# Reordering the first batch's loads and norms in a cross-covariance attention kernel with a folded feed-forward part

## The chip, the cores and the metric

The kernel runs on one core of a Trainium2 chip. The time is the device time of one execution in microseconds (us). Six runs of the kernel before have a median of 585.03 us (584.68 to 585.35). The profile was taken of one execution of 584.84 us, in which the core's span is 583.0 us; the rest, 1.84 us, lies around the span.

Names: PE is TensorE (matmul), PEld its weight load, ACT is ScalarE, DVE is VectorE, POOL is GpSimd, SP is SyncE. L207 is line 207 of the kernel before.

## The reference

Attention runs over channels, not tokens, for each of 4 batches of 5824 tokens and 256 channels; the feed-forward part has no nonlinearity beyond a product.

```python
qn = q / (np.linalg.norm(q, axis=1, keepdims=True) + 1e-06)   # norms over the tokens, one per channel
kn = k / (np.linalg.norm(k, axis=1, keepdims=True) + 1e-06)
s = kn.transpose(0, 2, 1) @ qn / tau                          # 256 x 256 per batch, tau = 1
a = softmax(s)                                                # over the last axis, 1e-9 added to the sum
x = (v @ a).reshape(B * S, D)
out = (((x @ w1) * (x @ w2)) @ w3) @ w_out
```

## The kernel before, in words

**Folding.** v @ a @ w1 is computed as v @ (a @ w1): for each batch the 256 x 256 softmax is multiplied into w1 and w2 (`fold`, L291, eight units of two matmuls, each evicted with the softmax's row factor by ACT, L302, or DVE, L304). Likewise w3 @ w_out is made once (`w_unit`). So the main loop over a batch's tokens has three matmul steps: a and b (`emit_ab`, L348), their product (ACT copies a, L360; DVE multiplies, L362), and the output (`emit_out`, L367). A batch has 12 chunks of 512 tokens (the last of 192), and eight feature blocks j per chunk. v must be transposed first: by DMA from SP, or, for the first two pieces of batch 0, on PE (L121), with a copy by ACT (L123) or DVE (L125).

**Scores.** q and k come in six pieces a batch: pieces of 8 slots of 128 tokens, the last of 5 slots and a remainder of 64 tokens. `load_piece` (L95) issues them on POOL's queue, which converts f32 to bf16. Four buffers each hold q and k (L63), so the fifth piece waits until PE is done with the first. For batch 0 nothing else can run yet: `first_scores` (L194) takes each slot with six matmuls, two for the scores G (L207, 256 columns), two for q^T q (L211) and two for k^T k (L215, 128 columns each); the last two give the squared norms on their diagonals. For batches 1 to 3 the scores are spread over the batch before by an agenda (`score_units`), with the squares taken by ACT and added up by DVE.

**Softmax units.** `soft_units` (L220) makes the norms, the row of k factors on all partitions, the scaled scores, the exponentials, the sums, and the folds. For batch 0: `norms_first` multiplies the squares by the identity (L225) and sums the rows (L227); `rnorm` takes the square root by Ln and Exp on ACT (L248, L249), adds 1e-6 and inverts on DVE (L250, L251); `row` (L256) spreads the k factors by an f32 matmul (L259) and an ACT copy (L265); `scaled` multiplies G by that row (L271) and ACT takes the exponential with the q factor as its scale (L274). For batches 1 to 3 `norms` adds two accumulators on DVE (L232), and `ss` sums over the partitions by four f32 matmuls of one column (L240).

**Order.** The order on each engine is the order in which the program emits; there is no scheduler. Batch 0 runs straight through (L401 to L436). After that, `make_agenda` (L461) gives each side job a due time on a clock of estimated PE time, and `run_due` emits what is due ahead of each `emit_ab` or `emit_out`. The softmax units of the next batch have their due times in L499. In batch 0 POOL issues q and k of a piece in turn, two pieces ahead of PE (L401, L415), then v, w1, w2, w3 and w_out (L417 to L427). The program lets POOL have eight loads under way: the ninth waits for the first to land, and so on.

Of the kernel before, what the change touches and what calls it, by code (L numbers as in the profile page):

```python
# [10 lines left out]
AF = mybir.ActivationFunctionType  # L11
ALU = mybir.AluOpType
F32 = DT.float32
BF16 = DT.bfloat16

P = 128
PIECE = 8
# [6 lines left out]
def kernel(  # L24
# [12 lines left out]
    nc = tc.nc  # L37

    B, N, C = q.shape
    T, D = out.shape  # L40
    F = moe_w1.shape[1]
# [6 lines left out]
    CT = C // P  # L48
    FT = F // P
# [24 lines left out]
    nc.vector.memset(ones_f, 1.0)  # L74
    ones_b = consts.tile([P, 1], BF16)
    nc.vector.memset(ones_b, 1.0)

    w12 = consts.tile([P, CT, 2, F], BF16)
    W_sb = consts.tile([P, FT, D], BF16)
# [12 lines left out]

    pieces = {}

    def load_piece(nm, n, pi, split=False):  # L95
        pool = v_pool if nm == "v" else qk_pool
        t = pool.tile([P, PIECE, C], BF16, tag=nm, name=f"{nm}_{n}_{pi}")
        main, left = qk_main[nm, n]
        g = LAST if pi == NP_ - 1 else PIECE
        if pi == NP_ - 1:  # L100
            if nm != "v":
                nc.gpsimd.memset(t[LEFT:, g, :], 0.0)
            nc.gpsimd.dma_start(out=t[:LEFT, g, :], in_=left)
        cuts = [0, g] if not split else [0, g // 2, g]
        for lo, hi in zip(cuts, cuts[1:]):
            nc.gpsimd.dma_start(out=t[:, lo:hi, :], in_=main[:, pi * PIECE + lo : pi * PIECE + hi, :])
        pieces[nm, n, pi] = t
# [83 lines left out]
                units.append((0.22 if part < 2 else 0.0, lambda pr=pr, part=part: pair_unit(pr, part)))  # L191
        return units

    def first_scores(pi):  # L194

        if pi == 0:
            G_tiles[0] = psum.tile([P, CT, C], F32, tag="G", name="G_0", bufs=1)
            G_tiles["sq"] = psum.tile([P, 2 * CT, P], F32, tag="out", name="sq_0", bufs=3)
        G, S = G_tiles[0], G_tiles["sq"]
        qt, kt = pieces["q", 0, pi], pieces["k", 0, pi]  # L200
        g = PIECE if pi < NP_ - 1 else LAST + 1
        for i in range(g):
            first = pi == 0 and i == 0
            last = pi == NP_ - 1 and i == g - 1
            for ct in range(CT):
                cs = slice(ct * P, (ct + 1) * P)
                nc.tensor.matmul(  # L207
                    G[:, ct, :], lhsT=qt[:, i, cs], rhs=kt[:, i, :],
                    start=(first and ct == 0), stop=(last and ct == CT - 1), skip_group_check=True,
                )  # L210
                nc.tensor.matmul(  # L211
                    S[:, ct, :], lhsT=qt[:, i, cs], rhs=qt[:, i, cs],
                    start=(first and ct == 0), stop=False, skip_group_check=True,
                )
                nc.tensor.matmul(  # L215
                    S[:, CT + ct, :], lhsT=kt[:, i, cs], rhs=kt[:, i, cs],
                    start=False, stop=(last and ct == CT - 1), skip_group_check=True,
                )

    def soft_units(n):  # L220
        st = {}

        def norms_first():
            d = work.tile([P, 2 * CT, P], F32, tag="sq", name="dg", bufs=2)
            nc.vector.tensor_mul(d, G_tiles["sq"], ident.unsqueeze(1).to_broadcast([P, 2 * CT, P]))  # L225
            ss = work.tile([P, 4], F32, tag="ss0", name="ss0", bufs=1)
            nc.vector.tensor_reduce(out=ss, in_=d, op=ALU.add, axis=mybir.AxisListType.X)  # L227
            rnorm(ss)

        def norms():  # L230
            a1 = work.tile([P, 2, C], F32, tag="acc1", name=f"acc1_{n}", bufs=1)
            nc.vector.tensor_add(a1, accs[n][:, 0], accs[n][:, 1])  # L232
            st["a1"] = a1

        def ss():
            m = psum.tile([P, 512], F32, tag="ab", name=f"ss_{n}", bufs=4)
            for w in range(2):
                for ct in range(CT):
                    i = w * CT + ct
                    nc.tensor.matmul(  # L240
                        m[:, i : i + 1], lhsT=st["a1"][:, w, ct * P : (ct + 1) * P], rhs=ones_f,
                        start=(i == 0), stop=(i == 3), skip_group_check=True,
                    )
            rnorm(m[:, :4])

        def rnorm(src):
            r = work.tile([P, 4], F32, tag="r", name=f"r_{n}", bufs=2)
            nc.scalar.activation(out=r, in_=src, func=AF.Ln)  # L248
            nc.scalar.activation(out=r, in_=r, func=AF.Exp, scale=0.5)  # L249
            nc.vector.tensor_scalar_add(r, r, 1e-6)  # L250
            nc.vector.reciprocal(r, r)  # L251
            if inv_tau != 1.0:
                nc.vector.tensor_scalar_mul(r[:, :CT], r[:, :CT], inv_tau)
            st["r"] = r

        def row():  # L256
            m = psum.tile([P, 512], F32, tag="ab", name=f"row_{n}", bufs=4)
            for ct in range(CT):
                nc.tensor.matmul(  # L259
                    m[:, ct * P : (ct + 1) * P],  # L260
                    lhsT=st["r"][:, CT + ct : CT + ct + 1].to_broadcast([P, P]), rhs=ident,
                    start=(ct == 0), stop=(ct == CT - 1), skip_group_check=True,
                )
            kr = work.tile([P, C], F32, tag="kr", name=f"kr_{n}", bufs=1)
            nc.scalar.copy(kr, m[:, :C])  # L265
            st["kr"] = kr

        def scaled():
            s = work.tile([P, CT, C], F32, tag="s", name=f"s_{n}", bufs=1)
# [21 lines left out]
        def fold(i):  # L291
# [11 lines left out]
            else:  # L303
                nc.vector.tensor_scalar_mul(dst, m, st["rs"][:, c1 : c1 + 1])  # L304

        head = [(0.0, norms_first)] if n == 0 else [(0.0, norms), (1.0, ss)]
        return (
            head + [(0.6, row), (0.0, scaled), (0.2, sums)]
            + [(0.43, lambda i=i: fold(i)) for i in range(8)]
        )  # L310


    clock = [0.0]
# [11 lines left out]
    def at(t, cost, fn):  # L325
        seq[0] += 1
        agenda.append((t, seq[0], cost, fn))
# [68 lines left out]
    def load_qk(n, pi):  # L396
        load_piece("q", n, pi)
        load_piece("k", n, pi)


    load_qk(0, 0)  # L401
    load_qk(0, 1)
    masks.make_identity(nc, ident)
    nc.vector.tensor_copy(ident_b, ident)
    w3T = [
# [4 lines left out]
    w3r = moe_w3.rearrange("(jh jl) l -> jl jh l", jl=P)  # L410
    w1r = moe_w1.rearrange("(ch cl) f -> cl ch f", cl=P)
    w2r = moe_w2.rearrange("(ch cl) f -> cl ch f", cl=P)
    for pi in range(NP_):
        if pi + 2 < NP_:
            load_qk(0, pi + 2)  # L415
        if pi + 2 == NP_:
            load_piece("v", 0, 0, split=True)  # L417
            for h in range(2):
                hs = slice(h * F // 2, (h + 1) * F // 2)
                nc.gpsimd.dma_start(out=w12[:, :, 0, hs], in_=w1r[:, :, hs])  # L420
                nc.gpsimd.dma_start(out=w12[:, :, 1, hs], in_=w2r[:, :, hs])
            load_piece("v", 0, 1)
            for h in range(2):
                js = slice(h * FT // 2, (h + 1) * FT // 2)
                nc.gpsimd.dma_start(out=w3_bf[:, js, :], in_=w3r[:, js, :])
            nc.gpsimd.dma_start(out=wout_sb, in_=moe_w_out.rearrange("(lh ll) c -> ll lh c", ll=P))
            load_piece("v", 0, 2)  # L427
        first_scores(pi)
    soft0 = soft_units(0)
    soft0[0][1]()  # L430
    transpose_half_on_pe(0, 0, 0, True)
    for _, fn in soft0[1:3]:
        fn()
    transpose_half_on_pe(0, 0, 1, False)
    for _, fn in soft0[3:8]:
        fn()  # L436

    def w3_transpose(jt):
        pe_transpose(
# [21 lines left out]
    def make_agenda(b):  # L461
# [2 lines left out]
        n = b + 1  # L464
        if b == 0:
            for i in range(4):
                at(0.3 + 0.6 * i, 0.43, soft0[8 + i][1])
            at(7.0, 0.5, lambda: transpose_half_on_pe(0, 1, 0, True))
            at(8.0, 0.5, lambda: transpose_half_on_pe(0, 1, 1, False))
            for jt in range(FT):  # L470
                at((12.0 if jt < 4 else 15.0) + jt, 0.5, lambda jt=jt: w3_transpose(jt))
                at(24.0 + jt, 0.87, lambda jt=jt: w_unit(jt))
            at(14.0, 0.0, lambda: transpose_piece(0, 2))
            loads = [("v", 0, 3, 14.0), ("v", 0, 4, 34.0), ("v", 0, 5, 54.0)]
            loads += [("qk", 1, pi, t) for pi, t in enumerate([22.0, 30.0, 40.0, 52.0, 66.0, 80.0])]
            loads += [("v", 1, pi, t) for pi, t in enumerate([96.0, 108.0, 122.0])]
            t0, t1 = 52.0, 120.0
        else:
            loads = [("v", b, pi, t) for pi, t in [(3, 1.0), (4, 20.0), (5, 34.0)]]
            t0, t1 = 16.0, 104.0  # L480
            if n < B:
                loads += [("qk", n, pi, t) for pi, t in enumerate([4.0, 12.0, 27.0, 44.0, 58.0, 72.0])]
                loads += [("v", n, pi, t) for pi, t in enumerate([84.0, 96.0, 108.0])]
# [12 lines left out]
        for i, (cst, fn) in enumerate(units):  # L496
            at(t0 + (t1 - t0) * i / len(units), cst, fn)
        soft = soft_units(n)
        ts = [t1 + 1.0, t1 + 4.0, t1 + 6.5, t1 + 8.5, t1 + 12.0] + [t1 + 13.0 + 0.9 * i for i in range(8)]  # L499
        for t, (cst, fn) in zip(ts, soft):  # L500
            at(t, cst, fn)
        agenda.sort()
# [50 lines left out]
```

## Time and profile before

| what | value |
|---|---|
| median of 6 runs | 585.03 us |
| profiled execution | 584.84 us, span 583.0 us |
| PE busy | 562.1 us (96% of the span) |
| DVE, ACT busy | 372.8 us (64%), 339.0 us (58%) |
| POOL's queue | 39.46 MB as written, 39.1% of 16 DMA engines |
| PE idle ahead of L207, waiting for k | 12.4 us in 4 waits |
| first score matmul, last score matmul of batch 0 | 8.80 us, 35.43 us |
| first fold matmul, first a matmul | 40.71 us, 43.99 us |

How to read it: the span is the time from the first instruction to the last. An engine's busy share says little where stages have different limits: here PE is busy nearly all the time from about 41 us on, and waits only in the first 41 us. Loads are shown by the bytes that they write (bf16), half of what they read. Rows of a timeline give the start, the length, the engine, the line, the operation and, in brackets, the idle time before it and what ended it. Rows with "xN" merge N instructions. A matmul's length includes its pipeline; the distance from start to start is what it costs.

### The profile page before, as it was taken

The page shows a single profiled execution, that of the slowest core. Times are in us where ns is not written, and L with a number is a line of the kernel's source. Part 1 is how long each engine was busy: PE and PEld are TensorE (multiplying, and loading weights), DVE is VectorE, ACT ScalarE, POOL GpSimd, SP SyncE. Part 2 cuts the span into 40 slices and gives each one's busy share as a digit, 9 for nine tenths or more (in the row PEclk, how much of TensorE's full clock was granted, in tenths as well). Part 3 has the DMA queues.
Part 4 walks back from the last instruction along what each step waited for, and adds up shares of the span by engine and source line. Part 5 has one row for each costly group of instructions (what it writes and reads, how often), then busy time and mean ns, then how long its engine had stood idle before and what let it go on. Part 6 is the DMA issues. An engine that isn't in the chain of part 4 may idle for free.

```text
span 583.0 us, 10194 instructions
## 1 busy us (share of the span) xinstructions
PE 562.1 (96%) x3836; PEld 363.2 (62%) x3840; DVE 372.8 (64%) x552; ACT 339.0 (58%) x617; POOL 68.5 (12%) x145
## 2 busy tenths in 40 slices
PE   3779999999999999999999999999999999999996
PEld 3654576766666666666665766666665765566555
DVE  0026644788877567778866567777876556555564
ACT  0026635677756576767755567777766545454454
POOL 3330111121100112002100112002100000000000
PEclk9999999999999999999999999999999999999999
DMA  8999879864644699754572599754564335401011
GB/s 167 212 208 186 132 145 209 166 137 122 134 108 73 147 202 182 148 109 98 134 145 73 114 198 181 149 138 94 127 135 101 81 80 140 91 38 73 37 69 54
DMA packets 65393, 74.85 MB, mean 128 GB/s; under 512 B 45760, under 2 KB 49344, under 8 KB 65344
## 3 DMA queue, kind: packets, MB, share of 16 engines
q0 software_dynamic: 14656, 39.46, 39.1%
q1 hardware_dynamic: 50688, 34.74, 21.7%
q8 instruction: 30, 0.49, 0.3%
q14 instruction: 19, 0.16, 0.1%
HBM read 78.91 MB, written 23.86 MB: 176 GB/s over the span
## 4 chain that ended last, share of the span: by engine, by line
PE 93%; DMA 4%; DVE 1%; ACT 1%; issue 1%; POOL 0%; ACTq 0%; POOLq 0%
PE o L376 28%; PE a L354 26%; PE b L354 26%; PE G L177 5%; DMA k<-in_k_dram 4%; PE fold L296 3%; PE w L449 1%; PE G L207 1%; DVE abs L362 1%; ACT as L360 1%; PE sq L211 1%; PE sq L215 1%; PE ss L240 0%; PE row L259 0%; ACT e L274 0%
## 5 line engine op out<-in xcount | busy, mean ns | idle before, releaser
L362 DVE TENSOR_TENSOR abs<-as,b 128x512 bf16<-128x512 bf16 (+1 forms) x384 | 252.5, 659 | 158.5 <-ACT as L360 144.0
L360 ACT CAST as<-a 128x512 bf16<-128x512 f32 (+1 forms) x384 | 215.7, 562 | 173.7 <-DVE abs L362 85.3
L376 PE MATMUL o<-W_sb,abs 128*128 128x256 bf16 x1472 | 221.3, 273 | 0.2 <-DVE abs L362 0.2
L354 PE MATMUL b<-vT,Wf 128*128 128x512 bf16 x704 | 209.5, 379 | 0.1
L354 PE MATMUL a<-vT,Wf 128*128 128x512 bf16 x704 | 209.5, 379 | 0.1
L354 PEld LDWEIGHTS <-Wf 128*128 128x128 bf16 x1536 | 148.8, 98 | 97.2 <-issue 1.4
L376 PEld LDWEIGHTS <-abs 128*128 128x128 bf16 x1472 | 143.4, 98 | 86.4 <-DVE abs L362 0.4
L186 DVE TENSOR_TENSOR acc<-acc,sq 128x1024 f32<-128x1024 f32 x66 | 80.4, 1219 | 0.4 <-ACT sq L174 0.4
L346 POOL COPY gate_t<-abs 1x1 bf16<-1x1 bf16 x39 | 15.5, 398 | 395.6 <-DVE abs L362 378.9
L177 PE MATMUL G<-k,q 128*128 128x256 bf16 x276 | 50.1, 273 | 0.0
L174 ACT ACTIVATE sq<-q 128x512 f32<-128x512 bf16 x66 | 41.8, 634 | 0.0
L174 ACT ACTIVATE sq<-k 128x512 f32<-128x512 bf16 x66 | 41.6, 631 | 0.0
L207 PE MATMUL G<-k,q 128*128 128x256 bf16 x92 | 22.7, 289 | 12.4 <-DMA k<-in_k_dram 12.4
L390 DVE COPY osb<-o 128x512 f32<-128x512 f32 x44 | 30.1, 684 | 0.4 <-PE o L376 0.4
L177 PEld LDWEIGHTS <-q 128*128 128x128 bf16 x276 | 27.0, 98 | 3.1
L389 ACT COPY osb<-o 128x512 f32<-128x512 f32 x44 | 25.8, 585 | 4.0 <-PE o L376 1.9
L248 ACT ACTIVATE r<-ss 128x4 f32<-128x4 f32 x4 | 0.7, 181 | 38.3 <-DVE ss L227 35.1
L211 PE MATMUL sq<-q 128*128 128x128 bf16 x92 | 21.2, 230 | 0.0
L215 PE MATMUL sq<-k 128*128 128x128 bf16 x92 | 21.2, 230 | 0.0
L225 DVE TENSOR_TENSOR dg<-sq,ident 128x512 f32<-128x512 f32 x1 | 0.7, 693 | 31.3 <-PE sq L215 31.3
L296 PE MATMUL fold<-w,e 128*128 128x512 bf16 x60 | 17.0, 406 | 0.4 <-issue 0.2
L302 ACT ACTIVATE Wf<-fold,rs 128x512 bf16<-128x512 f32 x16 | 11.0, 687 | 9.6 <-PE fold L296 7.7
(78 smaller groups left out, 198.1 us busy)
## 6 DMA issues: line engine op xcount, KB each, us to landing
out_dram<-osb SPq DMA_DIRECT2D x44, 512.0 KB, 2.9
q<-in_q_dram POOLq DMA_DIRECT2D x20, 512.0 KB, 6.0
k<-in_k_dram POOLq DMA_DIRECT2D x20, 512.0 KB, 8.8
v<-in_v_dram POOLq DMA_DIRECT2D x19, 512.0 KB, 5.2
w_bf<-in_moe_w_dram POOLq DMA_DIRECT2D x2, 1024.0 KB, 16.9
q<-in_q_dram POOLq DMA_DIRECT2D x4, 320.0 KB, 5.0
k<-in_k_dram POOLq DMA_DIRECT2D x4, 320.0 KB, 5.9
v<-in_v_dram POOLq DMA_DIRECT2D x4, 320.0 KB, 5.1
```

The costliest lines, as they stand in the source:

```text
L174: nc.scalar.activation(out=dst[:, :, part, :], in_=src[:, o : o + 2, :], func=AF.Square)
L177: nc.tensor.matmul(G[:, ct, :], lhsT=qt[:, i, ct * P : (ct + 1) * P], rhs=kt[:, i, :], start=(pr == 0 and part == 0 and ct == 0), stop=(pr ...
L186: nc.vector.tensor_add(accs[n], accs[n], sqs[0])
L207: nc.tensor.matmul(G[:, ct, :], lhsT=qt[:, i, cs], rhs=kt[:, i, :], start=(first and ct == 0), stop=(last and ct == CT - 1), skip_group_ch ...
L211: nc.tensor.matmul(S[:, ct, :], lhsT=qt[:, i, cs], rhs=qt[:, i, cs], start=(first and ct == 0), stop=False, skip_group_check=True,)
L215: nc.tensor.matmul(S[:, CT + ct, :], lhsT=kt[:, i, cs], rhs=kt[:, i, cs], start=False, stop=(last and ct == CT - 1), skip_group_check=True,)
L296: nc.tensor.matmul(m, lhsT=st["e"][:, c2, c1 * P : (c1 + 1) * P], rhs=w12[:, c2, w, h * 512 : (h + 1) * 512], start=(c2 == 0), stop=(c2 == ...
L354: nc.tensor.matmul(t[:, :n], lhsT=Wf[b][:, ct, w, j * P : (j + 1) * P], rhs=rhs_of(b, c, ct), start=(ct == 0), stop=(ct == CT - 1),)
L360: nc.scalar.copy(a_sb[:, :n], tiles[0][:, :n])
L362: nc.vector.tensor_mul(ab[:, :n], a_sb[:, :n], tiles[1][:, :n])
L376: nc.tensor.matmul(tl[s // 2][:, s % 2, :], lhsT=ab[:, off : off + P], rhs=W_sb[:, j, :], start=(j == 0 and s % 2 == 0), stop=(j == FT - 1 ...
L390: nc.vector.tensor_copy(o[:, 2:4, :], tl[1])
```

## The change

For batch 0, `first_scores` is replaced by `squares` and `products`, which take any range of slots. The loads run k0 (in two halves), k1, k2, q0, k3, q1, k4, q2, k5, q3, q4 (two halves), q5 (remainder, four slots, one slot): k is two pieces ahead of q. Then come w1 and w2 in halves with the halves of v0 between them, then v1, w3, w_out, v2 as before. The zeroing of the unused part of the last pieces moves from POOL to DVE. `busy(14)` ahead of everything and `busy(6)` behind the last products issue matmuls of 512 columns on a tile of zeros whose result is not used.

For all batches, the factors of k are made as a row at once: `k_row` multiplies a 128 x 128 matrix of ones with the squares (f32, 256 columns) and ACT takes Ln, Exp, Ln with 1e-6 added, and Exp of the 128 x 256 result. q keeps the column path, with 2 columns where 4 were. In batch 0, `k_row` stands between the two halves of piece q3. In batches 1 to 3, `k_row` and `q_sums` take the places of `ss` and `row`, both at nearly one point. In batch 0 the first transpose of v now stands behind the first four folds, and the second in the agenda.

```diff
-    def first_scores(pi):
...
+    def busy(k):
+        m = psum.tile([P, 512], F32, tag="ab", name=f"warm_{nc.get_next_instruction_name()}", bufs=4)
+        for _ in range(k):
+            nc.tensor.matmul(m, lhsT=warm[:, :P], rhs=warm, start=True, stop=True, skip_group_check=True)
+    def squares(nm, pi, slots, end=False):
...
+        for i in slots:
+            for ct in range(CT):
+                nc.tensor.matmul(S[nm][:, ct, :], lhsT=t[:, i, cs], rhs=t[:, i, cs],
...
+    def products(pi, slots, end=False):
...
+        for i in slots:
+            for ct in range(CT):
+                nc.tensor.matmul(G_tiles[0][:, ct, :], lhsT=qt[:, i, ct * P : (ct + 1) * P], rhs=kt[:, i, :],
...
-        def norms_first():
-            nc.vector.tensor_mul(d, G_tiles["sq"], ident.unsqueeze(1).to_broadcast([P, 2 * CT, P]))
...
+        def k_first():
+            d = work.tile([P, CT, P], F32, tag="sq", name="dk", bufs=2)
+            nc.vector.tensor_mul(d, S["k"], ident.unsqueeze(1).to_broadcast([P, CT, P]))
+            st["ksq"] = d.rearrange("p c t -> p (c t)")
+        def q_first():
+            d = work.tile([P, CT, P], F32, tag="sq", name="dq", bufs=2)
+            nc.vector.tensor_mul(d, S["q"], ident.unsqueeze(1).to_broadcast([P, CT, P]))
+            ss = work.tile([P, CT], F32, tag="ss0", name="ss0", bufs=1)
+            nc.vector.tensor_reduce(out=ss, in_=d, op=ALU.add, axis=mybir.AxisListType.X)
+            q_norm(ss)
...
+        def k_row():
...
+            nc.tensor.matmul(m[:, :C], lhsT=ones_pp, rhs=st["ksq"], start=True, stop=True)
...
+            nc.scalar.activation(out=kr, in_=m[:, :C], func=AF.Ln)
+            nc.scalar.activation(out=kr, in_=kr, func=AF.Exp, scale=0.5)
+            nc.scalar.activation(out=kr, in_=kr, func=AF.Ln, bias=eps_t)
+            nc.scalar.activation(out=kr, in_=kr, func=AF.Exp, scale=-1.0)
...
-        head = [(0.0, norms_first)] if n == 0 else [(0.0, norms), (1.0, ss)]
...
-            head + [(0.6, row), (0.0, scaled), (0.2, sums)]
+            head = [(0.0, k_first), (0.6, k_row), (0.0, q_first)]
...
+            head = [(0.0, norms), (0.5, k_row), (0.4, q_sums)]
...
+    busy(14)
+    load_piece("k", 0, 0, split=True)
+    load_piece("k", 0, 1)
...
+    load_piece("k", 0, 2)
+    squares("k", 0, lo)
+    squares("k", 0, hi)
+    squares("k", 0 + 1, range(PIECE))
+    for pi in range(NP_ // 2):
+        load_piece("q", 0, pi)
+        load_piece("k", 0, pi + 3)
+        squares("k", pi + 2, range(PIECE))
+        products(pi, range(PIECE))
+        squares("q", pi, range(PIECE))
+    load_piece("q", 0, 3)
+    load_piece("q", 0, 4, split=True)
+    load_piece("q", 0, 5, split=True)
...
+    squares("k", 5, range(LAST + 1), end=True)
     soft0[0][1]()
+    products(3, lo)
+    squares("q", 3, lo)
+    soft0[1][1]()
+    products(3, hi)
+    squares("q", 3, hi)
+    for sl in (lo, hi):
+        squares("q", 4, sl)
+        products(4, sl)
...
+    squares("q", 5, first)
+    products(5, first)
+    squares("q", 5, rest, end=True)
+    soft0[2][1]()
+    products(5, rest, end=True)
+    soft0[3][1]()
+    busy(6)
+    for _, fn in soft0[4:9]:
+        fn()
     transpose_half_on_pe(0, 0, 0, True)
...
+            at(4.0, 0.5, lambda: transpose_half_on_pe(0, 0, 1, False))
...
-        ts = [t1 + 1.0, t1 + 4.0, t1 + 6.5, t1 + 8.5, t1 + 12.0] + [t1 + 13.0 + 0.9 * i for i in range(8)]
+        ts = [t1 + 1.0, t1 + 3.5, t1 + 4.0, t1 + 8.0, t1 + 12.0] + [t1 + 13.0 + 0.9 * i for i in range(8)]
```

## The prediction

> **What bounds the kernel now.** I read the page first: PE is busy 96% of the span, so only work on PE, or a wait of PE, is worth time. Then the waits of PE: 12.4 us in four waits of L207 for k, all before 30 us. Then the chain of waits that ended last, from 12 to 46 us; its columns are start, length and what. It is the stretch that the change rebuilds:
>
> ```profile
> 15.52 13.74 DMA k<-in_k_dram
> ...
> 35.68 0.70 DVE dg L225
> 36.41 0.70 DVE ss L227
> 37.13 0.21 ACT r L248
> 37.37 0.21 ACT r L249
> 37.61 0.18 DVE r L250
> 37.81 0.19 DVE r L251
> 38.04 0.72 PE row L259 x4
> 38.79 0.38 ACT kr L265
> 39.20 0.44 DVE s L271
> 39.66 0.92 ACT e L274 x2
> 40.62 0.23 PE sum L281 x3
> 40.85 0.36 PE fold L296
> ```
>
> Two things are to be seen. Until k4 lands at 29.3 the loads set the pace; the four waits and the load rate of 203 to 217 GB/s in every window from 6 to 35 us say so. From 29.3 to 35.65 it is PE, with 14 slots left at 0.44 us; then 5.0 us of small steps follow, in which PE has little to do. The third thing is the clock, in windows of 3.4 us. The columns are the window, its length, busy time (and count) of PE, PEld, DVE, ACT and POOL, PE's granted clock, DMA share, GB/s:
>
> ```profile
> 20.28:23.69 3.41, 2.05 (x29) 1.83 (x27) 0.00 (x0) 0.00 (x0) 1.47 (x3) 1.00 1.07 213
> ...
> 37.34:40.75 3.41, 1.47 (x17) 1.20 (x18) 1.70 (x5) 2.38 (x5) 0.30 (x1) 1.00 1.19 215
> 40.75:44.17 3.42, 3.20 (x11) 1.23 (x11) 1.08 (x3) 1.37 (x2) 0.00 (x0) 0.51 1.09 208
> ```
>
> After a window with PE busy 43% (1.47 of 3.41) the clock is halved for about 3.4 us, while the folds run; after one with 60% it is not. Last, the timeline of PE in batch 1, where the other changed units stand:
>
> ```profile
> 169.12 0.95 PE L240 MATMUL ss<-ones_f,acc 128*128 128x1 f32 x8
> 169.93 0.59 PE L354 MATMUL a<-vT,Wf 128*128 128x512 bf16 x2
> ...
> 171.23 0.61 PE L259 MATMUL row<-ident,r 128*128 128x128 f32 x4
> 171.68 0.59 PE L354 MATMUL a<-vT,Wf 128*128 128x512 bf16 x2
> ```
>
> PE does not wait here, so what these units cost is the distance to the next start: 0.81 us for ss, 0.45 for row.
>
> **Loading.** The bytes up to the last of q and k are the same, so the last lands as before: the load of w_bf that waits for k5 is issued at 33.02 us, so k5 landed at about 32.95. Landings in units of a full piece: 2 at 8.8 us, 6 at 18.6, 8 at 24.4, 10 at 29.3. In the new order q0 is the 4th (about 13.7), q1 the 6th (18.6), q2 the 8th (24.2), k5 ends at 8.7, q3 at 9.7 (28.6), q4 at 10.7 (31.1), q5 by 32.95. Per slot, products take 0.22 us and squares of one tensor 0.11 (0.44 in all before: 0.22 + 0.11 + 0.11; a run of eight 128-column transposes starts every 0.056 us, so squares alone hold this pace). k's squares are out of the way early, so q3 finds PE free at 28.6. But then 22 slots are left at 0.33 = 7.3 us, and `k_row` between them. Its price: row's 128 f32 columns in two instructions take 0.45/2 = 0.22, so 256 take 0.22 (if weight loads set it) to 0.45; I take 0.43, as twice the columns. PE ends its last square of q at 28.6 + 7.3 + 0.4 - 0.2 (last products behind it) + 0.2 (its own length) = 36.25, against 35.65 before. So the new order **loses 0.6 us** here: q comes last, and q carries three quarters of PE's work. The finer last pieces gain nothing, as PE is behind the loads by then. POOL's queue: k4 waits for PE to finish the products of piece 0 (13.7 + 1.8 = 15.5), and q2 and all loads behind stand in line; k5 waits for products 1 (20.4). Data pending then lasts to 18.6 and 24.2. The first load needed about 2.7 us from issue (1.24) to full rate (about 4), so spare time is 0.4 and 1.1 us: no bubble, but near. The two halves' extra issues are 0.55 us each on POOL, which has spare time; zeroing on DVE (0.31, 0.34 on POOL) falls where DVE is idle. The 14 matmuls on zeros end at about 7 us at the latest (0.43 each at half clock from 1 us), when PE would wait for k0 anyway; k0's squares end two pieces ahead of need.
>
> **The softmax chain.** dg and ss halve their columns. By s (256 f32 columns, 0.42) they take 0.84 instead of 1.39: 0.54 less. Ln, Exp, add, reciprocal stay. row and kr leave the path: from the end of the reciprocal (38.0) to s (39.20) is 1.2 us; k's row is made from `k_row` at about 30, with four ACT operations of some 0.43 us (copy of the same form 0.37, L274 0.50), done by 32. s to the first fold stays 1.5 us. First fold: 40.71 + 0.6 - 0.54 - 1.2 = **39.56** (1.15 us earlier).
>
> **Folds to the main loop.** Before: 40.71 to the second a (45.70), 4.99 us, of it 3.4 at half clock. After, at full clock: four folds 1.73, transposes 0.45; ACT evicts fold 0 and fold 2 (0.69 each) and then copies vT (1.0), which ends near 42.9; a and b 0.87, fold 0.43, second a at 44.2. That is 1.45 us earlier. The second transpose, hidden before in the chain, now costs its 0.45 in the busy loop. Together batch 0 gains **1.0 to 1.1 us**. `busy(6)` is 1.3 us of PE from 36.45, in the gap; sum starts near 39.0, so there is 1.2 us of room. Were the chain shorter by more than that, these matmuls would delay sum one for one.
>
> The clock row decides the 3.4 us. After the change PE idles from about 37.7 to 39.5 but for 0.2 us of sums, so the worst window is busy 1.6 to 1.8 of 3.41, 47 to 53%: between the 43% that lost the clock and the 60% that kept it. I take kept, because in the losing window 1.2 of the 1.47 us were f32 rows and transposes, and here it is plain matmuls up to the gap. The Trainium skill, "TensorE: Matmul & The Clock Gate", section "Why this matters for your kernels", asks only for no idle gap above about 3 us between bursts; the trace contradicts it, as its longest gap there is 1.95 us and the clock was still lost. Section "Part 4: PE-mode transpose" of that page says that transposes don't count as busy in the same way, which fits the row. By the first rule the new gap of 1.8 us is safe and 583.6 stands; by the row taken at its worst (53% loses too) it would be 584.3 to 585.3.
>
> **Batches 1 to 3.** PE: ss 0.81 + row 0.45 = 1.26 before; after, `k_row` 0.43 and half of ss 0.40 = 0.83 (0.62 with the low price). But ACT now has four operations of 256 columns in line, then r's two, before the next copy of a: 4 x 0.43 + 0.45 = 2.2 us. Queued behind are the copy of a, DVE's product, and PE, which has two pairs of a and b ahead in PSUM. From the unit's start T: row visible at T + 0.63, ACT done at 2.8, copy 3.4, product 4.2; PE wants that buffer for its third b at 3.86, and waits to 4.2. Before, the same b started at T + 4.29. The gain is **0.1 us a batch**. Also norms' add ends at 167.93 in batch 1 and `k_row` is due one unit earlier than ss, at 167.82: 0.15 lost; in batches 2 and 3 it stands where ss stood, 0.76 us behind the add. Together 0.15 us gained; ends: 1.9 gained (0.64 each, no stall) to 1.0 lost (0.5 us an ACT operation and a second stall).
>
> **Sum.** 584.84 - 1.1 - 0.15 = **583.6 us**, against the profiled execution's own time; the median of the runs is 0.19 above that execution. Its own range is 582.2 to 584.5.
>
> **Rivals.**
> 1. The clock is lost again ahead of the folds. For: at worst 47%, and the window's place is not fixed to the kernel. Against: plain matmuls up to the gap. Folds and transposes (2.2 us) then take up to twice as long, partly under the wait for vT: 0.7 to 1.7 more, 584.3 to 585.3.
> 2. Slower: ACT's line in batches 1 to 3. If its four operations take 0.69 each, as ACT's 512-column evictions do, the third b waits to T + 5.24, 0.95 later than before, three times: 584.84 - 1.1 + 0.15 + 2.85 = 586.7. It decides in a batch from 0.45 us an operation on, where the chain passes T + 4.29, and outruns batch 0's gain from 0.53 on. Against: 256-column rows of ACT are 0.37 to 0.50. A price of 0.55 gives 585.1.
> 3. q is late. A half clock in the k phase (windows there are busy only 26 to 52%) puts products 0 at 17.3 instead of 15.5, k4's load behind the pending data, a bubble of 0.7 to 1.4 us, and all later landings with it; or half clock in the last 22 slots, up to 1.7. 584.3 to 585.3, and up to 587 with rival 1 on top.
> 4. The change does what it says but the row was not what bound: then only the clock counts; within the forecast's range.
>
> **Chances.** Forecast 0.58, rival 1 0.17, rival 2 0.11, rival 3 0.14. About 0.2% (1.17 us) is what a measurement of this kernel can tell from no change: below 583.67 counts as faster. The forecast lies at that edge; 0.42 of its 0.58 falls below, counting that a low price of `k_row` and an earlier q3 add gain. Same is 0.16 of it, 0.15 of rival 1, 0.03 of 2 and 0.07 of 3, together 0.41; slower is the rest of them, 0.02, 0.08 and 0.07, together 0.17. The range, 582.2 to 585.8, leaves out the worst of rivals 2 and 3.
>
> **What would show it.** First fold near 39.6; last square of q near 36.2, later than before; kr done by 32; granted clock 1.00 from 39 to 45; in batches 1 to 3 a wait of PE under 0.4 us behind `k_row`. Wrong if the clock row shows 0.50 there, if PE waits for q4 or q5, or if POOL's k4 is issued after 17 us.

## The result, and the profile after

| | before | after |
|---|---|---|
| median (range, runs) | 584.96 us (583.07 to 585.85, 37) | 586.26 us (585.30 to 587.76, 16) |
| profiled execution | 584.84 us, span 583.0 us | 586.16 us, span 584.3 us |

The ratio is 1.0025 with a 95% interval of 1.0018 to 1.0032: the change makes the kernel 1.3 us **slower**. The forecast was 583.6 us, and the time lies above its range of 582.2 to 585.8.

The chain of waits of the kernel after, for the stretch that was shown of before; start, length, what:

```profile
4.04 9.88 DMA q<-in_q_dram
13.96 3.59 PE G L237 x16
...
21.50 0.53 POOL k L117
22.03 0.54 POOL k L121
22.57 7.99 DMA q<-in_q_dram
30.61 1.05 PE G L237 x8
...
38.35 0.44 DVE dq L253
38.81 0.43 DVE ss L255
...
40.10 0.33 DVE s L297
40.46 0.92 ACT e L300 x2
41.42 0.23 PE sum L307 x3
41.65 1.75 PE fold L322 x8
```

Read it from the end. The softmax chain did what was foretold: from dq to the folds it has 3.3 us, where before had 5.2 from dg on, and `row` and `kr` are no longer links of it. But it starts at 38.35, 2.7 us later than dg did before. Going back, q3 starts at 30.61 (foretold 28.6), its load waits behind POOL's issue of k5 at 21.50 (L117, L121), and at the root stand products 0, the 16 matmuls of q0 with k0, 3.59 us long, where 16 matmuls at full clock take 1.9 (products 1 took 1.91). The windows of PE's clock say why; columns as in the prediction (window, length, PE, PEld, DVE, ACT, POOL, granted clock, DMA share, GB/s):

```profile
7.42:10.83 3.41, 1.07 (x16) 0.90 (x16) 0.00 (x0) 0.00 (x0) 0.00 (x0) 1.00 1.07 215
10.83:14.24 3.41, 2.16 (x18) 1.84 (x19) 0.00 (x0) 0.00 (x0) 0.00 (x0) 0.50 1.06 214
14.24:17.66 3.42, 3.42 (x19) 2.48 (x18) 0.00 (x0) 0.00 (x0) 0.00 (x0) 0.50 1.07 214
17.66:21.07 3.41, 3.41 (x49) 3.22 (x47) 0.00 (x0) 0.00 (x0) 1.07 (x2) 1.00 0.69 108
38.10:41.50 3.40, 1.93 (x14) 0.91 (x14) 1.83 (x6) 1.31 (x4) 1.44 (x2) 1.00 1.21 209
```

While only k comes in, PE has one short burst of squares per piece: 1.07 us busy in 3.41, 31%. The clock is halved from 10.83 to 17.66, and q0, which lands at 13.9 (foretold 13.7), meets a PE at half speed. In the fourth row the clock is whole again, but the load rate has fallen to 108 GB/s. The fifth row is the window ahead of the folds: 57% busy, and the clock is kept. The timeline of POOL joins the two (start, length, engine, line, operation, and in brackets the idle time before it and what ended it):

```profile
5.08 0.56 POOL L121 DMA_DIRECT2D q<-in_q_dram  x1
17.86 0.53 POOL L121 DMA_DIRECT2D k<-in_k_dram  x1 [12.22 <-PE G L237]
18.38 0.55 POOL L121 DMA_DIRECT2D q<-in_q_dram  x1
```

k4 takes the buffer of k0, and PE is done with k0 only when products 0 are: POOL stands 12.2 us, and issues k4 at 17.86, after the 17 us that the prediction named as its point of failure. By then the data pending is all but used up: the rate is 29 GB/s from 18 to 19 us. This is the pause (the prediction's bubble). q2 and all behind it stand in the same line. This agrees with the Trainium skill, "DMA: Bandwidth & Descriptors", section "Anatomy of one DMA — SWDGE (gpsimd) path", by which a transfer's wait is done on the engine that issues it, before it is handed on; the 12.22 us on POOL show it here.

Where the 1.3 us lie: the first a after the folds of batch 0 starts at 44.94 (43.99 before). Aligned by a (the start of the n-th matmul of a in one trace, less that of the n-th in the other), after is 1.13 us late at the end of the first eight chunks, and 1.21 at the end of the kernel. Batches 1 to 3 hold next to nothing.

### The profile page after: what moved, and what is told of

It is laid out like the page before. It is cut to its first block, busy times and chain, and to the rows that moved or that the text cites. A ratio compares the mean times of both kernels' runs of the same rounds, so it can differ in the third digit from the quotient of the medians.

```text
span 584.3 us, 10213 instructions
## 1 busy us (share of the span) xinstructions
PE 567.1 (97%) x3836; PEld 363.2 (62%) x3840; DVE 373.8 (64%) x564; ACT 343.3 (59%) x629; POOL 65.0 (11%) x140
## 4 chain that ended last, share of the span: by engine, by line
PE 91%; DMA 3%; DVE 2%; issue 1%; ACT 1%; POOL 1%; ACTq 0%; POOLq 0%
PE o L402 27%; PE a L380 26%; PE b L380 26%; PE G L192 5%; DMA q<-in_q_dram 3%; PE fold L322 2%; PE G L237 2%; PE w L500 1%; DVE abs L388 1%; ACT as L386 1%; PE sqq L225 1%; POOL k L121 0%; PE row L267 0%; DVE osb L416 0%; DVE acc L201 0%
## 5 line engine op out<-in xcount | busy, mean ns | idle before, releaser
L372 POOL COPY gate_t<-abs 1x1 bf16<-1x1 bf16 x39 | 12.4, 318 | 397.8 <-DVE abs L388 389.6
L192 PE MATMUL G<-k,q 128*128 128x256 bf16 x276 | 50.2, 273 | 0.0
L269 ACT ACTIVATE kr<-row 128x256 f32<-128x256 f32 x4 | 1.5, 383 | 33.2 <-PE row L267 33.2
L237 PE MATMUL G<-k,q 128*128 128x256 bf16 x92 | 13.2, 298 | 3.6 <-DMA q<-in_q_dram 3.6
L121 POOL DMA_DIRECT2D k<-in_k_dram x25 | 13.7, 550 | 13.0 <-PE G L237 12.2
L121 POOL DMA_DIRECT2D q<-in_q_dram x26 | 14.0, 542 | 5.3 <-ACT as L386 3.5
L121 POOL DMA_DIRECT2D v<-in_v_dram x24 | 12.9, 537 | 7.0 <-issue 4.0
```

What stands on the lines that cost most here:

```text
L192: nc.tensor.matmul(G[:, ct, :], lhsT=qt[:, i, ct * P : (ct + 1) * P], rhs=kt[:, i, :], start=(pr == 0 and part == 0 and ct == 0), stop=(pr ...
L237: nc.tensor.matmul(G_tiles[0][:, ct, :], lhsT=qt[:, i, ct * P : (ct + 1) * P], rhs=kt[:, i, :], start=(pi == 0 and i == 0 and ct == 0), st ...
```

## The experiments

The theory: the half clock of the k phase delays products 0, and through k0's buffer it stops the line of loads (rival 3 of the prediction). Against it stood: PE's lateness by itself, with the loads only a sign of it; the zeros and the new norms of batches 1 to 3 as costs of their own; and the order itself, q last, whatever the clock. Each ratio is to the kernel before, run beside it on the same chip (585.1 us in each group; e5 to e8 ran on one chip, the others on another). Differences between kernels are of their medians unless a trace is named.

### Keep the clock in the k phase (e1_fill)

```diff
     squares("k", 0, hi)
+    busy(8)
     squares("k", 0 + 1, range(PIECE))
+    busy(6)
...
         squares("k", pi + 2, range(PIECE))
+        if pi == 0:
+            busy(6)
```

> The changed kernel with 20 more matmuls on zeros, 8 behind k0's squares, 6 behind k1's and 6 behind k2's, where TensorE waits for loads. Theory (the half clock from 10.8 to 17.7 us makes the products of piece 0 end 1.8 us late, POOL issues k4 at 17.9 instead of 16, and the load queue runs dry from 18 to 20 us): granted clock 1.00 from 7 to 20 us, k4 issued near 16, q3 at 28.6 to 29.2 instead of 30.6, time 1.4 to 2.0 us below the changed kernel. Rival (the order itself starves the queue, as k4 waits for the products at any clock): k4's issue moves but loads still pause, gain under 0.6 us. Rival (q last makes TensorE the limit in the last 22 slots whenever q3 lands): last square of q stays near 38, no gain.

Measured: 587.67 us (585.77 to 590.71), ratio 1.0047 (1.0027 to 1.0068), 1.4 us above after; the intervals of the two ratios overlap, so what is clear is that it gains nothing. The expectation failed. Products 0 ran at full clock, but late, since the zeros stand ahead of them in PE's line. PE's and POOL's timelines of e1_fill:

```profile
14.79 1.92 PE L237 MATMUL G<-k,q 128*128 128x256 bf16 x16
```
```profile
17.01 0.54 POOL L121 DMA_DIRECT2D k<-in_k_dram  x1 [11.38 <-PE G L237]
```

k4's issue gained 0.85 us (17.01 against 17.86), which isn't enough: the rate from 18 to 20 us is 143 GB/s, better than 66 but still a pause. k5's was later (21.95 against 21.50), as PE waited 1.23 us for q1, until 19.73; then PE starved for data, lost the clock from 27.6 to 31.0, and q's products paid for it. So the clock, bought with zeros in PE's own line, is not the cure as long as a load hangs on it. In this order of loads no run has products 0 both on time and at full clock with the four buffers, so that the pause would then not come is argued, not shown.

### Take the loads off PE's progress (e2_kbufs)

k4 and k5 of batch 0 get memory that isn't needed until later (that of the w3 transposes), so that no load of k waits for products. The clock is left as it is.

```diff
-        t = pool.tile([P, PIECE, C], BF16, tag=nm, name=f"{nm}_{n}_{pi}")
+        if nm == "k" and n == 0 and pi >= 4:
+            t = w3T[0][:, 2 * (pi - 4) : 2 * (pi - 4) + 2].rearrange("p a (b h) c -> p (a b) (h c)", h=2)
+        else:
+            t = pool.tile([P, PIECE, C], BF16, tag=nm, name=f"{nm}_{n}_{pi}")
```

> The changed kernel with k4 and k5 of batch 0 in memory of their own (that of w3T, not used before 57 us), so that their loads wait for no products; the clock is left alone. Theory (what costs is the pause of the loads): no pause, q3 near 28.6, TensorE half a clock until 17.7 but with the slack of its later waits for q to catch up, time 1.6 to 2.1 us below the changed kernel. Rival (the half clock itself costs, by TensorE's own lateness): loads on time but the last square of q still at 37 to 38, gain under 0.6 us.

Measured: 584.61 us (584.35 to 584.79), ratio 0.9991 (0.9983 to 1.0000): 1.65 us below after (2.0 by the two ratios). PE's timeline of e2_kbufs has the slow product still in it, and q3 in time:

```profile
13.99 3.60 PE L240 MATMUL G<-k,q 128*128 128x256 bf16 x16 [0.82 <-DMA q<-in_q_dram]
...
28.86 1.05 PE L240 MATMUL G<-k,q 128*128 128x256 bf16 x8 [0.76 <-DMA q<-in_q_dram]
```

The window from 18 to 20 us, first of after, then of e2_kbufs, ends in the load rate: 66 against 209 GB/s.

```profile
18.00:20.00 2.00, 2.00 (x34) 1.93 (x31) 0.00 (x0) 0.00 (x0) 0.92 (x2) 1.00 0.57 66
```
```profile
18.00:20.00 2.00, 2.00 (x31) 1.99 (x29) 0.00 (x0) 0.00 (x0) 0.63 (x2) 0.82 1.03 209
```

q3 starts 1.75 us earlier than in after (28.86 against 30.61), and the folds with it (39.76 against 41.51). Aligned by a, the two stay 1.75 us apart to the end of the kernel. The last square of q starts at 36.28, so the rival, which kept it at 37 to 38, fails. The pause is the loss.

### Both together (e7_fillbufs)

e2_kbufs with the three `busy` of e1_fill.

> e2_kbufs with the 20 more matmuls on zeros of e1_fill. Theory (only the pause of the loads costs; the clock in the k phase does not, once no load hangs on it): within 0.4 us of e2_kbufs (584.61), up to 0.8 above if the zeros make TensorE late. Rival (the half clock itself is worth something): 0.8 us or more below e2_kbufs.

Measured: 584.60 us (584.43 to 586.09), ratio 0.9991 (0.9983 to 1.0000), the same as e2_kbufs. PE's timeline of e7_fillbufs:

```profile
14.97 1.92 PE L240 MATMUL G<-k,q 128*128 128x256 bf16 x16
...
29.01 1.05 PE L240 MATMUL G<-k,q 128*128 128x256 bf16 x8 [0.73 <-DMA q<-in_q_dram]
```

With buffers free the half clock of the k phase costs nothing: here products 0 start a microsecond later and run at full clock, and in both runs PE has caught up and waits some 0.75 us for q3. The half clock costs only through the load that waits for it.

### No zeros at all (e3_nozeros)

```diff
-    busy(14)
...
-    busy(6)
```

> The changed kernel without both groups of matmuls on zeros. Theory (the first 14 warm the clock for nothing, since it is lost again before q0; the 6 behind the products keep it for the folds): clock half from the first square to about 17 us as now, lost also at the folds, as the window there falls from 57% to under 40% busy; time 0.8 to 1.7 us above the changed kernel. Rival (the folds keep their clock without them): within 0.3 us of the changed kernel.

Measured: 589.22 us (586.59 to 590.52), ratio 1.0067 (1.0046 to 1.0088), 3.0 us above after: more than expected. Both `busy` earn their place in its trace. Without the first the clock is half until 18.66 (16 squares take 1.89 us, at full clock 1.07), products 0 start at 14.70, k4 is issued at 18.59 and the pause is longer (35 GB/s from 18 to 20 us); the first fold is 0.94 us later than in after, so these 14 did not warm the clock for nothing, as the expectation had it. Without the second the clock is lost at the folds, as PE's timeline shows: six fold matmuls take 2.77 us where eight take 1.89 in after, and the first a is 2.62 us later.

```profile
43.18 2.77 PE L322 MATMUL fold<-w,e 128*128 128x512 bf16 x6 [0.22 <-issue]
```

### The new norms of batches 1 to 3 alone (e4_rows, e9_oldrows)

e4_rows is the kernel before with only these units; batch 0 keeps its own:

```diff
-        head = [(0.0, norms_first)] if n == 0 else [(0.0, norms), (1.0, ss)]
+        head = [(0.0, norms_first), (0.6, row)] if n == 0 else [(0.0, norms), (0.5, k_row), (0.4, q_sums)]
...
-            head + [(0.6, row), (0.0, scaled), (0.2, sums)]
+            head + [(0.0, scaled), (0.2, sums)]
...
-        ts = [t1 + 1.0, t1 + 4.0, t1 + 6.5, t1 + 8.5, t1 + 12.0] + [t1 + 13.0 + 0.9 * i for i in range(8)]
+        ts = [t1 + 1.0, t1 + 3.5, t1 + 4.0, t1 + 8.0, t1 + 12.0] + [t1 + 13.0 + 0.9 * i for i in range(8)]
```

> The kernel before with only the new norms of batches 1 to 3 (ones matmul, four ScalarE operations, both units at one point, and the new due times); batch 0 as before. Theory (by the starts of the a matmuls these units changed 0.04 us a batch): within 0.3 us of the kernel before. Rival (ScalarE's line stalls TensorE in the batches, and that makes the slowdown): 1 us or more above the kernel before.

Measured: 585.98 us (584.05 to 586.65), ratio 1.0011 (1.0001 to 1.0022). Aligned by a, the three batches cost 0.18, 0.04 and 0.04 us more than before. In its profiled execution the clock was whole at the folds, and from the first fold to the second a it takes 3.39 us (41.18 to 44.57), where before takes 4.99: the clock at the folds weighs 1.6 us. (It was lost from 24.6 to 28.1 us instead. The first fold came 0.47 later than in before, so the whole of batch 0 is 1.13 us ahead.) So the same batch 0 can keep the clock at the folds or lose it.

e9_oldrows is the reverse, on the best version (e6_tail, below), with `ss`, `row` and their due times back:

> e6_tail with the norms of batches 1 to 3 as in the kernel before (ss, row and their due times); batch 0 as in e6_tail. If the starts of a in e4_rows read rightly (the new units cost 0.18, 0.04 and 0.04 us in the three batches), this is 0.25 us below e6_tail's 581.36: 581.0 to 581.2. If the prediction's account of these batches holds (0.15 us gained by the new units), it is 581.5. If ACT's line stalls PE as the slower rival said, it is 580.5 or less.

Measured: 581.02 us (580.76 to 581.41), ratio 0.9935 (0.9921 to 0.9948), against 581.36 (581.17 to 582.42) of e6_tail, run on another chip. The medians say 0.34 us for the old units. The two traces, aligned, end 0.09 us apart, e9_oldrows behind, with that distance already there before batch 1's units; but e9_oldrows has one pause of 0.26 us at 204.3 us, ahead of a product of batch 2's scores and of no known cause, that e6_tail has not. Set that aside, and the new units cost the 0.26 us that e4_rows showed. So the gain of 0.15 that was foretold isn't there, and a loss of about 0.3 us is likely, not shown. ACT's line of four does not stall PE by the 0.95 us of the slower rival.

### q no longer last (e5_even)

The loads of after in the order k0 q0 k1 q1 k2 q2 k3 q3 k4 q4 k5 q5, with the finer last pieces of q, the zeros and the norms kept; `k_row` stands behind k5's squares.

```diff
-    load_piece("k", 0, 0, split=True)
+    load_piece("k", 0, 0)
+    load_piece("q", 0, 0)
     load_piece("k", 0, 1)
+    load_piece("q", 0, 1)
...
     load_piece("k", 0, 2)
+    load_piece("q", 0, 2)
+    load_piece("k", 0, 3)
+    load_piece("q", 0, 3)
...
+    for pi in range(4):
+        if pi == 1:
+            load_piece("k", 0, 4)
+            load_piece("q", 0, 4, split=True)
+        if pi == 2:
+            load_piece("k", 0, 5)
+            load_piece("q", 0, 5, split=True)
+        squares("k", pi, range(PIECE))
         products(pi, range(PIECE))
         squares("q", pi, range(PIECE))
...
```

> The changed kernel with k and q loaded in turn again, k first: k0 q0 k1 q1 k2 q2 k3 q3 k4 q4 (halves) k5 q5 (parts); no load has to wait for late products, and only 6 slots of q are left when k5 lands. k_row stands behind k5's squares. All else as in the changed kernel. Theory (the order of the loads is what costs, by the pause and by q coming last): no pause, last square of q near 34.5 us instead of 38.1 (e2_kbufs: 36.4), time 1.0 to 2.0 us below e2_kbufs, 582.7 to 583.6. Rival (the k row is late in this order and sets the end of the chain): kr done after s could start, gain under 0.5 us on e2_kbufs.

Measured: 582.96 us (582.77 to 583.10), ratio 0.9964 (0.9952 to 0.9977), 3.3 us below after and 1.65 below e2_kbufs, which has no pause either. PE's timeline of e5_even:

```profile
34.82 0.27 PE L225 MATMUL sqq<-q 128*128 128x128 bf16 x2
...
38.40 1.89 PE L322 MATMUL fold<-w,e 128*128 128x512 bf16 x8
```

So k first costs twice: by the pause, and by what it leaves for the end. The last square of q starts at 34.82, against 36.28 in e2_kbufs, and the first fold at 38.40 against 39.76, 1.36 us earlier; aligned by a, that is the distance of the two traces at the end of the kernel too.

### The transposes ahead of the folds (e6_tail, e8_bufstail)

In after, PE waits 1.10 us for the copy of vT between the folds and the first a. e6_tail is e5_even with v0 loaded ahead of w1 and w2, both transposes back in the gap of the softmax chain, and four matmuls on zeros there instead of six; e8_bufstail is the same on e2_kbufs.

```diff
+    load_piece("v", 0, 0, split=True)
     for h in range(2):
...
-        load_piece("v", 0, 0, part=h)
...
     products(5, rest, end=True)
+    transpose_half_on_pe(0, 0, 0, True)
     soft0[3][1]()
-    busy(6)
+    transpose_half_on_pe(0, 0, 1, False)
+    busy(4)
     for _, fn in soft0[4:9]:
         fn()
-    transpose_half_on_pe(0, 0, 0, True)
...
-            at(4.0, 0.5, lambda: transpose_half_on_pe(0, 0, 1, False))
```

> e5_even with the tail of the kernel before: v0 loaded ahead of w1 and w2, and both its transposes on TensorE between the last products and the folds, with 4 matmuls on zeros instead of 6. Theory (in the change the first transpose and ScalarE's copy of it keep the first a matmul waiting 1.1 us, and the second costs 0.45 us in the busy loop): 1.2 to 1.8 us below e5_even, unless w2 lands late for the folds (then 0.5). Rival (the wait only moves to the folds' evictions): within 0.4 us of e5_even.

> e2_kbufs with the tail of e6_tail. Theory as there: 1.2 to 1.8 us below e2_kbufs (584.61), so 582.8 to 583.4; rival: within 0.4 us of it.

Measured: e6_tail 581.36 us (581.17 to 582.42), ratio 0.9940 (0.9927 to 0.9952), 1.6 us below e5_even; e8_bufstail 582.86 us (582.52 to 583.20), ratio 0.9963 (0.9951 to 0.9975), 1.75 below e2_kbufs. PE's timeline of e6_tail:

```profile
35.08 0.61 PE L136 MATMUL tr_I-462_463<-ident_b,v 128*128 128x128 bf16 x8
35.53 0.61 PE L136 MATMUL tr_I-479_480<-ident_b,v 128*128 128x128 bf16 x8
...
38.27 1.89 PE L322 MATMUL fold<-w,e 128*128 128x512 bf16 x8
39.99 0.59 PE L380 MATMUL a<-vT,Wf 128*128 128x512 bf16 x2
```

The transposes start at 35.1 and 35.5, where PE waits for the exponentials, and a follows the folds at once: 39.99, where after has 44.94. This version beats both kernels, before by 3.8 us on its chip.

### The row back on the path (e10_rowback)

e6_tail, but batch 0 makes k's factors by columns, and `row` (defined as in the kernel before) behind the reciprocal:

```diff
-            q_norm(ss)
+            rnorm(st["ss0"])
...
-            head = [(0.0, k_first), (0.6, k_row), (0.0, q_first)]
+            head = [(0.0, k_first), (0.0, lambda: None), (0.0, q_first)]
...
         def scaled():
+            if n == 0:
+                row()
```

> e6_tail with the factors of k in batch 0 made as before: the columns of k are summed early, but Ln, Exp, add and reciprocal run on all four columns, and the row by f32 matmul and ACT copy stands behind them again. If the row was on the path, as the prediction's term of 1.2 us says, the first fold comes 1.0 to 1.2 us later than in e6_tail (38.27 there) and the time is 582.4 to 582.6. If ACT's copy of vT, which in e6_tail ends just as the scaled scores are there, held the path anyway, it is under 0.5 us later: below 581.9. If the longer gap on PE loses the clock ahead of the folds, up to 1.7 us more: 583.3 to 584.3.

Measured: 582.49 us (582.04 to 582.62), ratio 0.9958 (0.9943 to 0.9973), 1.1 us above e6_tail. The clock stayed whole at the folds, so the third case did not come. The chain of waits has the row as two links again, and the folds start at 39.30 against 38.27. The row weighs a little more than that: without `k_row` ahead of it on PE the chain starts 0.31 us earlier (34.75 against 35.06), and from there to the first fold it takes 4.55 us against 3.21, 1.34 more.

```profile
36.34 0.19 DVE r L290
36.66 0.70 PE row L298 x4
37.38 0.38 ACT kr L304
37.79 0.44 DVE s L322
```

## Why the prediction was wrong

**The step that failed** is in "Loading": "k4 waits for PE to finish the products of piece 0 (13.7 + 1.8 = 15.5)" and "spare time is 0.4 and 1.1 us: no bubble, but near". The 1.8 is a price at full clock, taken in a stretch whose clock I had myself put in doubt under rival 3. Products 0 took 3.59, k4 was issued at 17.86, and the bubble came. e2_kbufs shows the price by removing the bubble and leaving the slow products: 1.65 us by the medians, 1.75 by q3's start and by every a behind it.

**Rival 3** named the mechanism and its place (products 0 at 17.3, k4 behind the pending data) and gave it a chance of 0.14. Its price, 0.7 to 1.4, was too low: 1.65 to 1.75. Its second half, the clock lost in the last 22 slots, did not come.

**The sum.** The forecast was 1.25 us below the profiled execution of before, and the last a is 1.21 us above it, 2.46 apart. Of these the pause is 1.75. The other 0.7 can be read in e2_kbufs, which has no pause:

- q3 starts at 28.86, not 28.6; the second a then stands at 44.48, not 44.2: 0.3.
- The second transpose of v takes 0.60 in the loop by the end of the first eight chunks (0.75 after the second chunk, 0.15 of it given back), not 0.45: 0.15.
- Batches 1 to 3 cost 0.07 in e2_kbufs and 0.08 in after, where a gain of 0.15 was foretold: 0.2. The ACT operations are 0.38, 0.42, 0.51 and 0.42 us, as priced (0.43), and the wait on the norms' add in batch 1 came as priced (0.2 us for 0.15). What fails is the gain set against them.

e2_kbufs, then, is the case that was foretold, and its last a is 0.55 us ahead of before's, and its profiled execution, 584.61 us, is 0.2 us below that of before (its span 0.5, 582.5 against 583.0) and just above the forecast's own range (582.2 to 584.5): without the pause the change is worth a few tenths, not 1.25.

**Right**, in the absence of a pause, were: the 0.6 us that q last loses (the last square of q ends at 36.56 in e2_kbufs, where 36.25 was foretold and before has 35.65; 0.26 of these 0.9 is q3's lateness); the first fold at 39.56 (39.76), so the 0.54 of the halved dg and ss; the row off the path, priced at 1.2 (1.1 by the medians of e10_rowback, 1.34 by its chain); `k_row` at 0.43 (0.44 from start to start in batch 2, 0.48 in batch 0); that finer last pieces gain nothing (PE waits for neither q4 nor q5); and the clock kept at the folds with a window of 47 to 53% foretold and 57% found. That rested on `busy(6)`: e3_nozeros loses it. The reason given for it, plain matmuls in place of f32 rows and transposes, is not borne out: e4_rows has before's rows and transposes there and kept the clock, after windows of 50 and 56%. One sign was missed without harm: kr was to be done by 32, and is at 34.45 (32.7 in e2_kbufs), long before s needs it.

**The skill's rule** against the row: the prediction weighed the idle gap of about 3 us of "TensorE: Matmul & The Clock Gate", section "Why this matters for your kernels". The k phase speaks against it once more: no idle stretch of PE in the window of 31% reaches 2 us, and the clock is lost. The same section's advice to keep PE busy for 4 us first is not contradicted, but did not carry through the k phase: after the 14 matmuls on zeros the clock was whole, and lost again at 10.83.

**Not settled.** What share of a window decides the clock. A clock lost in the traces comes back after 3.41 us or twice that. With windows counted in steps of 3.41 us from the clock's own changes, which puts before's losing window at 37.41 to 40.82 and 45%, the traces divide cleanly within their first 50 us: a whole clock was lost after windows busy 21 (e3_nozeros), 31 (after, e8_bufstail), 35 (e5_even), 36 (e4_rows), 39 (e1_fill), 41 (e2_kbufs) and 45% (before), and kept after 50 (e4_rows), 51 (e9_oldrows), 52 (e1_fill, e3_nozeros), 53% (after) and all above. The edge lies between 45 and 50% here; no run moved a window across it by itself. To get the clock back took more: in the second row of the windows above, after was 63% busy at half clock, and the clock stayed half for one window more. Why e1_fill's runs spread so far (585.77 to 590.71) was not followed up.

## What to carry to other kernels

When loads run through a few buffers in one in-order queue, the time at which PE frees the oldest buffer is part of the load schedule: price it at the clock that PE will have in that stretch, not at full clock, and compare it with the data still pending. Products that took 1.7 us longer (3.59 against 1.91) moved every load behind them, and the end of the kernel by 1.75. And when one operand is brought first, ask how much work the other leaves for the end: even order, with the same chain behind it, was 1.65 us better than k first without its pause (1.36 by the aligned traces).

## What the runs showed of the hardware that was not expected

- A slow clock without any cost: with buffers free, products 0 at 3.60 us and at full clock gave the same 584.6 us (e2_kbufs, e7_fillbufs).
- Matmuls on a tile of zeros keep the clock: with 20 of them in the k phase products 0 took 1.92 us instead of 3.59 (e1_fill, e7_fillbufs), and without the 14 and 6 of the change the kernel was 3.0 us slower (e3_nozeros).
- A load line that stood still takes its time to flow again: after the issue of k4 at 17.86 the rate was 66 GB/s from 18 to 20 us, and 197 from 20 to 22.
